# A new order of steps in the four later chunks and in the front of an mLSTM cell with an exact-GELU feed-forward

## The chip, the cores and the metric

The kernel runs on one core of one Trainium2 chip. The metric is the device time of one execution in microseconds (us). A core has five engines with a queue each, which run in the order of their own queue and wait for each other through semaphores: TensorE (PE, with its weight loads listed as PEld), VectorE (DVE), ScalarE (ACT), GpSimd (POOL) and SyncE (SP), which here issues the DMAs.

## The reference

Two blocks follow each other. The first is an mLSTM cell over 4 batches, 8 heads, 768 steps and a head dimension of 40, the second a feed-forward with exact GELU over all 3072 tokens of 8 x 40 = 320 features and 2048 hidden features, in float32.

```python
for t in range(S):                                   # B=4, H=8, S=768, D=40
    m_new = np.maximum(f_gate[:, :, t] + m, i_gate[:, :, t])
    f_stab, i_stab = np.exp(f_gate[:, :, t] + m - m_new), np.exp(i_gate[:, :, t] - m_new)
    C = f_stab * C + i_stab * outer(v_t, k_t)
    n = f_stab * n + i_stab * k_t
    denom = np.maximum(np.abs(n . q_t), 1.0)
    y[:, :, t] = sigmoid(o_gate[:, :, t]) * (C @ q_t) / denom
x = y.transpose(0, 2, 1, 3).reshape(3072, 320)
h = x @ w_in                                         # 320 -> 2048
out = (0.5 * h * (1.0 + erf(h / sqrt(2)))) @ w_out   # 2048 -> 320
```

## The kernel before, in words

**Tiling.** The 768 steps are cut into six chunks of 128 steps for all four batches. Inside a chunk the recurrence is computed in matrix form: scores of queries and keys, weighed by a mask of decays, times the values, plus what the state carried over from the chunks before gives. The 512 tokens (4 x 128) of a chunk then go through the feed-forward: an up-projection into 16 rows of 128 hidden features each, GELU, and a down-projection that adds up 16 rows of products. Float32 products are taken as three faster products each (a rounded part, the rest against it, and a low part, `x_hi`, `x_rest`, `x_low`, and likewise for weights and for GELU's results). A row of the down-projection is 3 parts x 4 batches = 12 matmuls (line 991); the up-projection is lines 966 and 977.

**What sets the order.** The program is put under a manual schedule: steps are emitted by `play` from strings of words, and each engine runs its instructions in the order of emission. A word is a letter and, mostly, a number (a batch, a row or a quarter). There is one string for the front (`FRONT`: loading, the cells of chunks 0 and 1, the conversion and splitting of weights, and the feed-forward of chunk 0), one for chunk 1 (`SECOND`), one for chunks 2, 3 and 4 (`LATER`) and one for chunk 5 (`LAST`). While a later chunk's feed-forward runs on TensorE, the cell of the next chunk, and the masks and transposes of the one after it, are threaded between its products.

**Letters of a later chunk.** `U`, `u` up-projection of a quarter and its 64-row remainder; `g`n GELU of row n (ACT lines 984 and 985, then DVE lines 986 and 987); `d`n the products of row n; `E` the results of the chunk before (line 1015). Cell steps, with number 0 to 3 for the next chunk's batches and 4 to 7 for those of the chunk behind it: `M` mask (POOL line 474), `W` weights (exp, ACT line 500), `G` gate (ACT line 506), `D` weighed values `vw` (line 539), `K`, `Q` transposes of keys and queries (DVE line 512), `S` scores of two batches (PE line 568, DVE line 574), `C` reading the state for two batches (PE line 621), `h` updating it (PE line 632, DVE lines 639 and 647, POOL line 643), `V` values (PE line 674, DVE line 678), `Y` finish (DVE from line 685), `t` a copy that the transposes need (line 699), `X` transposes of y (PE line 708) with `x_hi` (ACT line 718), `R` the rest and low parts (DVE lines 727 and 728). `L`, `B`, `J`, `O`, `j`, `o` and `+` issue DMAs on SP; `Z`, `a`, `b` split weights.

**Letters of the front.** `K` and `J` are the two halves of converting a piece of weights (`K`: ACT lines 404 and 405; `J`: DVE lines 416 and 419 and the load of a later piece); `m w g t s c v y x` are mask, weights, gate, turn (transposes, PE line 530, copied by ACT line 533), scores (PE line 552, DVE line 555), carry (PE line 590), values (PE line 656), finish and transposes of y for chunk 0, `M W G T S C V Y X R` the same for chunk 1; `I4` sets four matmuls that keep the clock up, issued at the next bank that is not read; `A`, `U`, `f` are parts of chunk 0's up-projection, `i` the split of its weights (line 756), `u` of its x; `F` is the next row of chunk 0's products (line 888: four float32 matmuls, or 12 of the faster kind for a row whose GELU result was split by `z`, lines 873 to 875); `a`, `b` split the output weights (lines 935 and 943); `(`, `)`, `[`, `p`, `r`, `e` and `+` prepare chunk 2's keys and queries.

In the mechanism, a step waits where its operands or its buffer or bank are not ready, and everything behind it on the same engine waits with it. GELU's result `g_whole` has two buffers, so a row's GELU waits for the DVE's second operation of the row two before it. Scores of two batches (`S`) take the banks that the GELU of four rows has just read.

Of the kernel before, what the change touches and what calls it, by code (L numbers as in the profile page):

```python
# [23 lines left out]


FRONT = """
    O0 L0 k1 P0 E L1 L2 t0 P1 k7 K w0 g0 N s0 w1 O1 O3 D k4 t1 P2 w2 c0 v0 J y0 Q s1 L3 O2 K d w3 q t2 L4 P3 v1
    g1 c1 J y1 s2 K x0 t3 x1 v2 g2 O4 J B4 g3 c2 y2 s3 B5 K x2 K L5 J T0 K v3 A y3 M1 x3 c3 G0 M0 H O7 O6 O5 J
    J i5 u0 L6 u1 K W0 J W1 I4 A K S0 T1 C0 J i6 V0 i7 u2 G2 K U M2 L7 S1 J G1 K U i8 W2 J i9 C1 T2 K
    M3 f2 S2 V1 Y0 T3 J Y1 C2 e W3 K K K J S3 J C3 f3 K X0 J K R0 J K J V2 K Y2 J J K  # L30
    K V3 X1 J K r F J K (0 )0 F J K F K J F X2 G3 F J K F Y3 R1 J K F p + + + + J F J a10,2 b10,2 z10 a12 b12 F X3 z11 F a13,3 b13,3 z12 F z13 [1 F B8 z14 F B9 R2 z15 F R3 B10 B11 F a8 b8 a9 b9 F"""
CELL = "MWGVYXRKQDCSht"

HI_AT = {3: ("w_out3", 0), 8: ("w_out3", 2), 4: ("w_out0", 0), 5: ("w_out0", 1), 6: ("w_out2", 0), 7: ("w_out2", 1), 9: ("f0", 0)}
# [1 line left out]
for at, first, key in ((HI_AT, 10, "h0"), (LO_AT, 10, "h1"), (HI_AT, 13, "b0"), (LO_AT, 13, "b1"), (HI_AT, 0, "b2"), (LO_AT, 0, "b3")):  # L36
    at.update((first + i, (key, i)) for i in range(3))
LATER = """
 U0 u0 E0 E1 E2 E3 K1 Q1 L2 D0 D1 C0 h0 M2 M3 g0 g1 g2 g3 +
 U1 u1 g4 d0 g5 d1 g6 d2 g7 S0 d3 K2 Q2 L3 W2 W3 G0 G1 G2 G3 +  # L40
 U2 V0 V1 u2 g8 d4 g9 K3 Q3 B4 B5 J0 J1 d5 g10 d6 g11 S2 L4 d7
 U3 u3 + M4 M5 Y0 Y1 D2 D3 K4 W4 W5 g12 t0 d8 g13 t1 d9 g14 X0 X1 R0 d10 g15 R1 C2 h2 O0 O1 d11 V2 V3 Y2 t2 B6 J2 d12 Y3 t3 Q4 L5 B7 d13 X2 X3 R2 d14 R3 d15 + O2 O3"""

SECOND = """
 U0 u0 j2 o0 o1 K1 Q1 L2 M0 M1 D0 D1 W0 W1 a0,3 b0,3 a3 b3 a4,2 b4,2 a6,2 b6,2 C0 h0 M2 M3 g0 g1 g2 g3 o2 o3 + +
 U1 u1 Z Z Z g4 d0 g5 d1 g6 d2 g7 S0 d3 K2 Q2 L3 W2 W3 G0 G1 G2 G3 Z Z +
 U2 V0 V1 u2 + g8 d4 g9 K3 Q3 B4 B5 J0 J1 d5 g10 d6 g11 S2 L4 d7
 U3 u3 + M4 M5 Y0 Y1 D2 D3 K4 W4 W5 g12 t0 d8 g13 t1 d9 g14 X0 X1 R0 d10 g15 R1 C2 h2 O0 O1 d11 V2 V3 Y2 t2 B6 J2 d12 Y3 t3 Q4 L5 B7 d13 X2 X3 R2 d14 R3 d15 + O2 O3"""

LAST = """  # L50
 U0 u0 E0 E1 E2 E3 g0 g1 g2 g3 U1 u1 g4 d0 g5 d1 g6 d2 g7 d3 
# [1056 lines left out]
```

## Time and profile before

| | us |
|---|---|
| median of 3 runs | 438.67 (437.14 to 439.19) |
| profiled execution, its own time | 438.46 |
| its span | 436.7 |
| TensorE busy | 427.3 (98%) |
| VectorE busy | 296.0 (68%) |
| ScalarE busy | 277.3 (63%) |
| GpSimd busy | 48.8 (11%) |
| granted TensorE clock | 1.00 of full speed |

The profile is of one execution; its times are counted from the start of the span. A line of the profile's page or of a query names the kernel's line, the engine, the operation and the tiles (out<-in). "waited for" and "<-" name what ended an idle time. "issue" is idle time for which the trace shows no cause. In the kernel's own terms the front takes up to about 118 us, the four chunks from there to about 380 us and the last chunk the rest.

### The profile page before, as it was taken

What the parts mean: (1) busy time and instruction counts of PE and PEld (TensorE: products, weight loads), DVE (VectorE), ACT (ScalarE), POOL (GpSimd) and SP (SyncE); (2) the same over time, 40 slices, a digit from 0 to 9 for tenths busy, and PEclk for the clock granted to TensorE, in tenths of its full rate; (3) what the DMA queues carried; (4) which work ended last, traced back from release to release, by engine and by line L of the source; (5) the groups of instructions that cost most, each with busy time, mean ns of one, the idle gap of its engine ahead of it and who ended that gap; (6) DMA issues with size and microseconds to landing.
All of it is one profiled execution on the core that took longest, in us unless ns stands there. A gap on an engine that the chain in (4) does not pass through costs nothing.

```text
span 436.7 us, 13291 instructions
## 1 busy us (share of the span) xinstructions
PE 427.3 (98%) x5472; PEld 374.6 (86%) x5472; DVE 296.0 (68%) x680; ACT 277.3 (63%) x595; POOL 48.8 (11%) x77
## 2 busy tenths in 40 slices
PE   8989999999999999999999999999999999999996
PEld 7777888877988899988899988899988889979986
DVE  8797687797888697747597747597746586533330
ACT  4989999856889985228785229785247715243441
POOL 3001030000430041030041030040010000000000
PEclk9999999999999999999999999999999999999999
DMA  7999994577791592662492653571561400010001
GB/s 151 220 214 243 233 256 87 138 211 179 229 154 56 106 176 60 115 179 50 84 187 42 123 158 60 117 134 32 110 156 17 62 2 2 22 42 2 1 2 60
DMA packets 162268, 48.83 MB, mean 112 GB/s; under 512 B 147776, under 2 KB 155232, under 8 KB 162208
## 3 DMA queue, kind: packets, MB, share of 16 engines
q1 hardware_dynamic: 161888, 47.65, 50.1%
q8 instruction: 43, 0.70, 0.6%
q10 hardware_dynamic: 320, 0.33, 0.2%
q14 instruction: 17, 0.14, 0.1%
HBM read 43.84 MB, written 9.37 MB: 122 GB/s over the span
## 4 chain that ended last, share of the span: by engine, by line
PE 73%; DVE 2%; ACT 2%; DMA 1%; issue 1%; ACTq 0%
PE po L991 31%; PE pu L966 24%; PE pu L977 7%; PE ps L568 3%; PE pf L621 2%; PE ph L674 1%; PE po L888 1%; PE po L674 1%; PE px L708 1%; DMA bits<-in_moe_w_out_dram 1%; PE pf L632 1%; DVE pow L416 1%; DVE w_out L419 0%; ACT w_out_part L935 0%; ACT g_part L873 0%
## 5 line engine op out<-in xcount | busy, mean ns | idle before, releaser
L991 PE MATMUL po<-w_out_part,g_parts 128*128 128x320 f32 x960 | 140.7, 303 | 0.0
L991 PEld LDWEIGHTS po<-w_out_part,g_parts 128*128 128x128 f32 x960 | 131.6, 189 | 5.9 <-issue 4.6
L986 DVE TENSOR_TENSOR g_parts<-g_whole,g_parts 128x512 fp32r<-128x512 f32 x80 | 57.0, 713 | 58.1 <-ACT g_parts L985 56.0
L984 ACT ACTIVATE g_whole<-pu 128x512 f32<-128x512 f32 x80 | 47.1, 589 | 74.2 <-PE pu L977 63.7
L985 ACT ACTIVATE g_parts<-g_whole 128x512 fp32r<-128x512 f32 x80 | 50.5, 631 | 8.3 <-PE po L991 5.1
L474 POOL TENSOR_SCALAR_AFFINE_SELECT W<-W 128x1024 f32<-128x1024 f32 (+2 forms) x20 | 21.7, 1088 | 189.2 <-DMA W<-M_d 154.4
L500 ACT ACTIVATE W<-W,aT 128x128 f32<-128x128 f32 x128 | 38.8, 389 | 0.3
L987 DVE CAST g_parts<-g_whole 128x512 fp32r<-128x512 f32 x80 | 36.2, 453 | 0.0
L699 ACT COPY far<-ob 128x128 f32<-128x128 f32 x16 | 4.6, 290 | 32.9 <-DVE ob L690 32.9
L966 PE MATMUL pu<-x_hi,w_in_hi 128*128 128x512 f32 x80 | 24.2, 384 | 0.0
L966 PE MATMUL pu<-x_hi,hi_first 128*128 128x512 f32 x80 | 24.0, 381 | 0.1
L966 PE MATMUL pu<-x_rest,hi_first 128*128 128x512 f32 x80 | 23.8, 379 | 0.0
L966 PE MATMUL pu<-x_rest,w_in_hi 128*128 128x512 f32 x80 | 23.8, 379 | 0.0
L966 PE MATMUL pu<-x_low,w_in_lo 128*128 128x512 f32 x80 | 23.8, 379 | 0.0
L966 PE MATMUL pu<-x_low,w_in 128*128 128x512 f32 x80 | 23.8, 379 | 0.0
L888 PE MATMUL po<-w_out,g 128*128 128x320 f32 x80 | 22.0, 432 | 0.0
L404 ACT ACTIVATE sig<-bits 128x320 f32<-128x320 f32 (+1 forms) x26 | 15.2, 586 | 10.4 <-issue 6.1
L574 DVE TENSOR_TENSOR W<-ps,W 128x256 f32<-128x256 f32 (+1 forms) x48 | 17.7, 414 | 4.2 <-PE ps L568 3.2
L888 PEld LDWEIGHTS po<-w_out,g 128*128 128x128 f32 x80 | 15.0, 190 | 5.9
L639 DVE TENSOR_TENSOR far<-pf,gT 128x164 f32<-128x164 f32 x32 | 8.4, 319 | 16.1 <-PE pf L632 11.7
L416 DVE SCALAR_TENSOR_TENSOR pow<-sig,pow 128x320 uint32<-128x320 uint32 (+1 forms) x26 | 15.4, 592 | 4.3 <-ACT pow L405 4.3
L1015 ACT ACTIVATE o_sb<-po 128x320 f32<-128x320 f32 x20 | 7.5, 443 | 16.7 <-PE po L991 16.7
(196 smaller groups left out, 778.9 us busy)
## 6 DMA issues: line engine op xcount, KB each, us to landing
W<-M_d SPq DMA_DIRECT2D x16, 512.0 KB, 6.5
bits<-in_moe_w_in_dram SPq DMA_DIRECT2D x20, 256.0 KB, 4.2
bits<-in_moe_w_out_dram SPq DMA_DIRECT2D x16, 320.0 KB, 4.6
blocks<-kq_d SPq DMA_DIRECT2D x32, 128.0 KB, 3.5
ob<-in_o_gate_dram SPq DMA_DIRECT2D x24, 160.0 KB, 4.1
out_dram<-o_sb SPq DMA_DIRECT2D x36, 80.0 KB, 2.0
wide<-M_d SPq DMA_DIRECT2D x4, 512.0 KB, 4.8
kq_d<-in_k_dram SPq DMA_DIRECT2D x6, 320.0 KB, 4.6
```

What stands on the lines that cost most here:

```text
L416: nc.vector.scalar_tensor_tensor(out=p, in0=s, scalar=3, in1=p, op0=OP.logical_shift_left, op1=OP.bitwise_or)
L474: nc.gpsimd.affine_select(out=x, in_=x, compare_op=OP.is_ge, fill=1.0e30, base=base, pattern=[[0, H], [1, x.shape[2]]], channel_multiplier=-1)
L500: nc.scalar.activation(out=W[n][:, h, :], in_=src, func=AF.Exp, scale=-1.0, bias=aT[:, self.c, r:r + 1])
L574: nc.vector.tensor_tensor(out=w[r, :, t], in0=ps[i][hip][r, :, t], in1=w[r, :, t], op=OP.mult)
L888: nc.tensor.matmul(to, xs[k][:, b * L:(b + 1) * L], w, start=(n == 0 and k == 0), stop=(n == NF - 1 and k + 1 == len(xs)), skip_group_chec ...
L966: nc.tensor.matmul(in_pairs(pus[i][e]), w3(at[k])[n][:, e, i * P:(i + 1) * P], in_turns(x3[n][:, k, :]), start=(n == 0 and k == 0), stop=F ...
L977: nc.tensor.matmul(in_pairs(pus[i][e]), w3(r)[n][h, p % 2, i * P:(i + 1) * P], in_turns(x3[n][h, NX, :]), start=False, stop=(n == 2), skip ...
L984: nc.scalar.activation(out=whole, in_=self.pus[n // 4][n % 4 // 2][n % 2], func=AF.Gelu)
L985: nc.scalar.activation(out=hi, in_=whole, func=AF.Copy, scale=PART)
L986: nc.vector.tensor_tensor(out=rest, in0=whole, in1=hi, op=OP.subtract)
L987: nc.vector.tensor_copy(out=low, in_=whole)
L991: nc.tensor.matmul(in_pairs(self.po[t]), x[:, t * L:(t + 1) * L], in_turns(w), start=(n == 0 and k == 0), stop=(n == NF - 1 and k == 2), s ...
```

## The change

Two of the strings get a new order from a given place on, and one throughout; no step is added or dropped, and no function changes.

- In the four later chunks the update `h2` is followed at once by the values `V3 V2` (before: `h2 O0 O1 d11 V2 V3`), the gelu `g15` and `R1` change turns, and the last transposes are spread, `d13 X2 d14 X3` in place of `d13 X2 X3 R2 d14 R3`, so that `R2 R3` come together. `Q3` and `K3` go ahead of `g9`; `Y1 D3 Y0` and `t1`, `t0` change turns.
- In chunks 2 to 4 also the first two quarters: the results of the chunk before (`E`) are spread between the steps, `D1 M2 D0 C0 M3 h0` replaces `D0 D1 C0 h0 M2 M3`, `S0` goes ahead of `g7`, and `G3 G1 G2 G0` ahead of `W3 W2`.
- The front is the same up to `v1 g1 c1 J y1 s2 K x0 t3 x1 v2 g2`; from there its cell steps, conversions, loads and splits come in another order. Among others `c2` follows `g2` directly, `I4` comes after `S0 C0`, `T2` before `i9`, and among the rows `F` the splits `z10`, `z11` and `z12` come one row earlier and the order of `Y3`, `R1`, `X2`, `X3` and of the copies `+` is new.

```diff
@@ -24,11 +24,12 @@
 
 
 FRONT = """
-    O0 L0 k1 P0 E L1 L2 t0 P1 k7 K w0 g0 N s0 w1 O1 O3 D k4 t1 P2 w2 c0 v0 J y0 Q s1 L3 O2 K d w3 q t2 L4 P3 v1
-    g1 c1 J y1 s2 K x0 t3 x1 v2 g2 O4 J B4 g3 c2 y2 s3 B5 K x2 K L5 J T0 K v3 A y3 M1 x3 c3 G0 M0 H O7 O6 O5 J
-    J i5 u0 L6 u1 K W0 J W1 I4 A K S0 T1 C0 J i6 V0 i7 u2 G2 K U M2 L7 S1 J G1 K U i8 W2 J i9 C1 T2 K
-    M3 f2 S2 V1 Y0 T3 J Y1 C2 e W3 K K K J S3 J C3 f3 K X0 J K R0 J K J V2 K Y2 J J K
-    K V3 X1 J K r F J K (0 )0 F J K F K J F X2 G3 F J K F Y3 R1 J K F p + + + + J F J a10,2 b10,2 z10 a12 b12 F X3 z11 F a13,3 b13,3 z12 F z13 [1 F B8 z14 F B9 R2 z15 F R3 B10 B11 F a8 b8 a9 b9 F"""
+    O0 L0 k1 P0 E L1 L2 t0 P1 k7 K w0 g0 N s0 w1 O1 O3 D k4 t1 P2 w2 c0 v0 J y0 Q s1 L3 O2 K d w3 q t2 L4 P3 v1 g1
+    c1 J y1 s2 K x0 t3 x1 v2 g2 c2 O4 J B4 y2 B5 s3 g3 K L5 J T0 x2 K K M1 v3 A y3 c3 M0 G0 x3 H J O6 O5 J O7 u0
+    L6 u1 K i5 W0 J W1 A K S0 C0 I4 T1 G2 J i6 u2 U i7 V0 K M2 S1 J G1 M3 L7 K U C1 i8 J W2 T2 i9 K f2 Y0 S2 V1
+    T3 J Y1 C2 K e W3 K J K S3 J C3 f3 K X0 J K J K K R0 J K V2 Y2 J J J K K V3 (0 X1 K F G3 J )0 J
+    K F J r F J F F X2 + R1 K K p F J Y3 + F + J z10 a12 K F a10,2 b10,2 J + b12 z11 F a13,3 b13,3 z12 F F X3 z13 F
+    B8 z14 F B9 R2 z15 F [1 R3 F a8 B10 B11 a9 b9 F b8"""
 CELL = "MWGVYXRKQDCSht"
 
 HI_AT = {3: ("w_out3", 0), 8: ("w_out3", 2), 4: ("w_out0", 0), 5: ("w_out0", 1), 6: ("w_out2", 0), 7: ("w_out2", 1), 9: ("f0", 0)}
@@ -36,16 +37,15 @@
 for at, first, key in ((HI_AT, 10, "h0"), (LO_AT, 10, "h1"), (HI_AT, 13, "b0"), (LO_AT, 13, "b1"), (HI_AT, 0, "b2"), (LO_AT, 0, "b3")):
     at.update((first + i, (key, i)) for i in range(3))
 LATER = """
- U0 u0 E0 E1 E2 E3 K1 Q1 L2 D0 D1 C0 h0 M2 M3 g0 g1 g2 g3 +
- U1 u1 g4 d0 g5 d1 g6 d2 g7 S0 d3 K2 Q2 L3 W2 W3 G0 G1 G2 G3 +
- U2 V0 V1 u2 g8 d4 g9 K3 Q3 B4 B5 J0 J1 d5 g10 d6 g11 S2 L4 d7
- U3 u3 + M4 M5 Y0 Y1 D2 D3 K4 W4 W5 g12 t0 d8 g13 t1 d9 g14 X0 X1 R0 d10 g15 R1 C2 h2 O0 O1 d11 V2 V3 Y2 t2 B6 J2 d12 Y3 t3 Q4 L5 B7 d13 X2 X3 R2 d14 R3 d15 + O2 O3"""
+ U0 E0 K1 E1 E2 Q1 E3 u0 L2 D1 M2 D0 C0 M3 h0 g0 g1 g2 g3 + U1 u1 g4 d0 g5 d1 g6 d2 S0 g7 K2 d3 Q2 L3 G3 G1 G2 G0 W3 W2
+ + U2 V0 V1 u2 g8 Q3 d4 K3 g9 B4 d5 B5 J0 J1 d6 g10 g11 S2 L4 d7 U3 + u3 M4 M5 D2 Y1 D3 Y0 K4 W4 W5 d8 g12 t1 g13 t0 d9 g14
+ X0 X1 R0 d10 R1 C2 h2 O0 g15 O1 V3 V2 Y2 d11 t2 B6 J2 d12 Y3 Q4 t3 L5 B7 d13 X2 d14 X3 R2 R3 + O2 O3 d15"""
 
 SECOND = """
- U0 u0 j2 o0 o1 K1 Q1 L2 M0 M1 D0 D1 W0 W1 a0,3 b0,3 a3 b3 a4,2 b4,2 a6,2 b6,2 C0 h0 M2 M3 g0 g1 g2 g3 o2 o3 + +
- U1 u1 Z Z Z g4 d0 g5 d1 g6 d2 g7 S0 d3 K2 Q2 L3 W2 W3 G0 G1 G2 G3 Z Z +
- U2 V0 V1 u2 + g8 d4 g9 K3 Q3 B4 B5 J0 J1 d5 g10 d6 g11 S2 L4 d7
- U3 u3 + M4 M5 Y0 Y1 D2 D3 K4 W4 W5 g12 t0 d8 g13 t1 d9 g14 X0 X1 R0 d10 g15 R1 C2 h2 O0 O1 d11 V2 V3 Y2 t2 B6 J2 d12 Y3 t3 Q4 L5 B7 d13 X2 X3 R2 d14 R3 d15 + O2 O3"""
+ U0 u0 j2 o0 o1 K1 Q1 L2 M0 M1 D0 D1 W0 W1 a0,3 b0,3 a3 b3 a4,2 b4,2 a6,2 b6,2 C0 h0 M2 M3 g0 g1 g2 g3 o2 o3 + + U1 u1 Z Z Z g4
+ d0 g5 d1 g6 d2 g7 S0 d3 K2 Q2 L3 W2 W3 G0 G1 G2 G3 Z Z + U2 V0 V1 u2 + g8 Q3 d4 K3 g9 B4 d5 B5 J0 J1 d6 g10 g11 S2 L4
+ d7 U3 + u3 M4 M5 D2 Y1 D3 Y0 K4 W4 W5 d8 g12 t1 g13 t0 d9 g14 X0 X1 R0 d10 R1 C2 h2 O0 g15 O1 V3 V2 Y2 d11 t2 B6 J2 d12 Y3 Q4
+ t3 L5 B7 d13 X2 d14 X3 R2 R3 + O2 O3 d15"""
 
 LAST = """
  U0 u0 E0 E1 E2 E3 g0 g1 g2 g3 U1 u1 g4 d0 g5 d1 g6 d2 g7 d3
```

## The prediction

> **What bounds the kernel now.** I read the page's busy times first, then the table by stage, then PE's waits ahead of 113 us, then the chain through one later chunk.
>
> ```profile
> PE 427.3 (98%) x5472; PEld 374.6 (86%) x5472; DVE 296.0 (68%) x680; ACT 277.3 (63%) x595; POOL 48.8 (11%) x77
> ```
> ```profile
> core 0: us, PE busy (x) PEld busy (x) DVE busy (x) ACT busy (x) POOL busy (x), PEclk, DMA share, GB/s
> 20.00:40.00 20.00, 18.15 (x361) 15.03 (x359) 18.05 (x48) 17.73 (x40) 0.00 (x0) 1.00 0.99 229
> 40.00:60.00 20.00, 19.62 (x210) 15.91 (x211) 14.86 (x25) 19.89 (x44) 3.31 (x3) 1.00 1.07 233
> ```
> ```profile
> 84.00:120.00 36.00, 35.35 (x281) 28.18 (x269) 30.44 (x64) 25.20 (x53) 4.77 (x5) 1.00 0.70 193
> ```
> ```profile
> 184.00:250.00 66.00, 66.00 (x931) 59.28 (x930) 44.96 (x106) 39.38 (x86) 10.53 (x14) 1.00 0.54 110
> ```
> TensorE sets the time: 98% busy, at a granted clock of 1.00 in every stage. The columns after the length are PE, weight loads, DVE, ACT, POOL. A later chunk (184 to 250) has no PE idle at all, so a new order there can save only what PE spends in its own switches; it can, however, create waits that are not there now. The front is different: between 20 and 40 PE is idle for 1.85 us, between 84 and 120 for 0.65, and between 40 and 60 ACT is full (19.89 of 20) and the DMA engines too (1.07).
>
> The waits of PE between 25 and 113 us, and the one DMA wait of ACT that bears on them (engine, line, what it waited for: us, times, longest):
> ```profile
> PE pf L590 <- DVE vw L539: 0.7, 1, 0.7
> PE po L888 <- DVE g_part L874: 0.6, 2, 0.4
> PE px L708 <- DVE y_rest L699: 0.5, 1, 0.5
> PE ps L552 <- ACT qT L533: 0.4, 1, 0.4
> ```
> ```profile
> ACT sig L404 <- DMA bits<-in_moe_w_in_dram: 1.0, 1, 1.0
> ```
> These 2.2 us are all that the front's order can win by visible waits. The change adds and removes no work: all matmuls, activations with their table loads, vector operations and DMAs are the same, in another order on each engine, so the sum below holds waits and switches only. It is made against the profiled execution's own 438.46 us (span 436.7 and 1.76 around it), 0.21 under the median of the three runs, 438.67.
>
> **Change, part 1: the tail of the four later chunks** (chunks 1 to 4, one text for chunk 1, one for 2 to 4). The chain of chunk 2 between the products of rows 8 and 15, and a run of three rows from chunk 4:
> ```profile
> 231.63 3.46 PE po L991 x24
> 235.09 0.66 PE px L708 x6
> 235.74 1.63 PE po L991 x12
> 237.38 1.07 PE pf L621 x64
> 238.45 0.74 PE pf L632 x32
> 239.19 1.83 PE po L991 x12
> 241.02 1.51 PE ph L674 x117
> 242.53 3.46 PE po L991 x24
> ```
> ```profile
> 246.69 3.26 PE po L991 x24
> ```
> ```profile
> 330.13 5.09 PE po L991 x36
> ```
> A row of products is 12 matmuls of L991: 1.63 us behind transposes (L708), 1.83 behind cell matmuls (L621, L632, L674). The 0.20 more is the switch. Before: rows 8-9, X0 X1, 10, read and update (C2 h2), 11, V2 V3, 12-13, X2 X3, 14-15. After: rows 8-9, X0 X1, 10, C2 h2 V3 V2, 11-12-13, X2, 14, X3, 15. One entry from cell matmuls goes: 1.83 + 3.46 + 3.26 = 8.55 becomes 5.09 + 1.63 + 1.63 = 8.35. The six transposes fall into two threes, which I cost at nothing. That is 0.20 a chunk, **0.8 us over four**; below, zero if the split transposes give it back, above, 1.2 if V behind h2 also loses a switch of 0.1.
>
> What waits for what: V3 and V2 now come one row (1.83 us) earlier. Their matmuls need W; what the DVE makes of them in place needs `far` of the update. The groups that carry this (all chunks; busy us, mean ns):
> ```profile
> L639 DVE TENSOR_TENSOR far<-pf,gT 128x164 f32<-128x164 f32 x32 | 8.4, 319 | 16.1 <-PE pf L632 11.7 <-PE pf L621 4.4
> L727 DVE TENSOR_TENSOR x_rest<-px,x_hi 128x384 fp32r<-128x384 f32 x20 | 11.0, 552 | 2.9 <-ACT x_hi L718 2.8
> L728 DVE CAST x_low<-px 128x384 fp32r<-128x384 f32 x20 | 10.9, 547 | 0.0
> L718 ACT ACTIVATE x_hi<-px 128x384 fp32r<-128x384 f32 x20 | 8.9, 487 | 2.1 <-PE px L708 1.9
> L987 DVE CAST g_parts<-g_whole 128x512 fp32r<-128x512 f32 x80 | 36.2, 453 | 0.0
> ```
> Four `far` operations are 1.3 us of DVE, beside V's own 1.51 us on PE, and the DVE is freer there than before: gelu row 15's two vector operations (0.65 for L986, shown below, and 0.45) move behind them, and they are not wanted before row 15's product, at least two rows (3.4 us) later. What V adds in place is only read by the finish Y2, which therefore starts no later, and X3 follows it as before. At the chunk's end only row 15 (1.63 us) lies between X3 and the next up-projection. Its operands follow in the order of their use, x_hi after 0.49 us, x_rest after 0.55 more and x_low after 0.55 more: 1.59. They are there when row 15 ends; I cost this at nothing, and without the cover it would be the second and third of these, 1.1 us.
>
> There is one wait which no dependency explains, in chunk 1's V2 V3:
> ```profile
> 176.69 0.35 issue
> ```
> "issue" means that PE waited for nothing that the trace records. It is 0.35 us once in four chunks; it may move or go (-0.35), or the longer stream of small matmuls (96 + 128, now without products between) may bring it into each of four chunks (+1.4). I take 0.
>
> [...]
>
> **Part 2: third quarter (U2).** The transposes K3 and Q3 (L512, on DVE) move from behind gelu row 9's vector work to ahead of it. DVE, ACT, POOL and PE of chunk 2:
> ```profile
> 219.31 0.70 DVE L512 STREAM_TRANSPOSE kT<-blocks 128x512 f32<-128x512 f32 x1
> 219.94 0.67 DVE L512 STREAM_TRANSPOSE qT<-blocks 128x512 f32<-128x512 f32 x1
> 220.53 0.65 DVE L986 TENSOR_TENSOR g_parts<-g_whole,g_parts 128x512 fp32r<-128x512 f32 x1
> ```
> ```profile
> 221.44 1.58 DVE L986 TENSOR_TENSOR g_parts<-g_whole,g_parts 128x512 fp32r<-128x512 f32 x1
> ```
> ```profile
> 219.55 0.58 ACT L984 ACTIVATE g_whole<-pu 128x512 f32<-128x512 f32 x1
> ```
> ```profile
> 221.27 1.20 POOL L474 TENSOR_SCALAR_AFFINE_SELECT W<-W 128x1024 f32<-128x1024 f32 x1 [25.43 <-ACT g_parts L985]
> ```
> ```profile
> 221.56 1.57 PE L568 MATMUL ps<-qT,kT 64*64 64x128 f32 x64
> ```
> The gelu of row 11 (219.55) reuses the buffer that row 9's L987 frees; that comes later by the two transposes' pitch, 220.53 - 219.31 = 1.22 us. So it ends at 219.55 + 0.58 + 1.22 = 221.35, and S2, whose first matmuls reuse the banks that the gelus empty, begins at 221.56. A margin of 1.4 us becomes 0.2. That costs nothing by these rows; but a DVE operation beside the POOL's mask took 1.58 instead of 0.65, so if the mask moves onto row 9's pair, S2 stalls by up to 2 x 0.93 - 0.2 = 1.7 us a chunk. I put +0.3, a sixth of that, for one chunk of four being touched lightly.
>
> [...]
>
> **Part 3: first and second quarters.** S0 goes ahead of row 7's vector work, the G steps change turns with no added table load, and on POOL the masks M2, M3 go ahead of the state's decay in h0.
> ```profile
> 192.11 0.93 POOL L643 TENSOR_TENSOR state<-state,dec 128x164 f32<-128x164 f32 x2 [8.21 <-PE pf L621]
> ```
> ```profile
> L474 POOL TENSOR_SCALAR_AFFINE_SELECT W<-W 128x1024 f32<-128x1024 f32 (+2 forms) x20 | 21.7, 1088 | 189.2 <-DMA W<-M_d 154.4
> ```
> POOL was idle for 8.21 us before that decay, and two masks of 1.20 fit in it if their loads have landed; the profile's largest wait of POOL is for these loads (154.4 of 189.2 us idle before L474), so this is not sure. If a load lands less than 1.2 us ahead of the decay, the decay is late by up to one mask. Zero, bounded by 0 and +1.2 in all.
>
> **Part 4: the front.** C2 now follows g2 directly, so vw (L539) runs on the DVE ahead of J's pair: the 0.7 at L590 goes. The y_rest wait (0.5) moves with s3 and x2. But all ACT work between the bits it waits 1.0 us for at 32 us and T1's copies at 55 is the same set, and ACT is full in that stretch; S1 waits for the last of those copies (L552 on L533 in the waits above). So what PE wins before 55 us becomes a longer wait at S1. I take 0, between -1.2 (if ACT's bits come earlier too) and +0.6 (the loads of that stretch are DMA-bound and change turns with the gate loads O4 to O7).
>
> From 84 us the F rows have the split rows 10 to 12. PE and the chain:
> ```profile
> 107.50 0.93 PE L888 MATMUL po<-w_out_part,g_part 128*128 128x320 f32 x4
> 108.70 3.53 PE L888 MATMUL po<-w_out_part,g_part 128*128 128x320 f32 x24 [0.27 <-DVE g_part L874]
> 112.61 0.68 PE L888 MATMUL po<-w_out_part,g_part 128*128 128x320 f32 x3 [0.38 <-DVE g_part L874]
> ```
> ```profile
> 102.29 2.98 issue
> ```
> 28 matmuls took 112.61 - 107.50 = 5.11 us; at 5.09 / 36 = 0.141 each they need 3.96. So 1.15 us is lost, more than the 0.6 which the waits show. The cause lies earlier: ACT stood 2.98 us after 102.29 because the next weight conversion needs a DVE step that is queued behind Y3, itself behind a gate on ACT, and R1. After the change these come apart: R1 goes behind an earlier J, Y3 behind four more rows, and the splits z10, z11, z12 each move one row earlier. With that idle gone, what was ready at 112.61 is ready at 109.6, and PE without waits would want it at 107.50 + 24 x 0.141 = 110.9. The wait goes whole: **-1.15**, at least -0.6 (what shows as waits). What would be late next is chunk 1's first up-projection, whose X3 comes after row 10 instead of before row 11; its cover is five rows of 12 x 0.141 = 1.70 us.
>
> Sum: -0.8 - 1.15 + 0.3 + 0 = -1.65 us; 438.46 - 1.65 = 436.8.
>
> **The rivals.** (a) *Faster:* the early front's 1.2 us are kept, the tails give 1.2 and the idle issue goes: -1.2 - 1.2 - 1.15 - 0.35 = -3.9, **434.6**. For it: two waits go for certain. Against: ACT at 19.89 of 20.
>
> (b) *No gain:* the split rows find another late input (weights' conversion is DMA-fed; the DMA share is 0.70 there) and keep 0.6 of their loss, and the split transposes eat the tails' 0.8: -0.5, **438.0**. In this case the change moves work but not PE.
>
> (c) *Slower:* S2 waits for row 11's gelu in all four chunks, since the mask's release by its DMA falls on row 9's DVE pair. At one operation stretched whole and one by half, 1.4 - 0.2 = 1.2 us each, four times, +4.8; with the -1.15 and -0.8 kept that is +2.85, **441.3**. It decides from a delay of 0.2 us upward, and outweighs the gains from 0.5 us a chunk. For it: the margin is one short operation. Against: the mask began 2 us behind row 9's place (221.27 against 219.31) in chunk 2.
>
> **How the numbers follow.** The forecast has 0.47, (a) 0.24, (b) 0.14, (c) 0.15. About 0.5%, 2.19 us, is what a measurement of this kernel can tell from no change: faster below 436.3, slower above 440.65. The forecast's own range is 435.6 to 438.0 (tails 0 to 1.2, split rows 0.6 to 1.15, S2 0 to 1); a third of it lies below 436.3. Faster: 0.24 + 0.16 = 0.40. Same: 0.31 + 0.14 = 0.45. Slower: 0.15. The range for 8 in 10 takes in (a) and stops short of (c)'s middle: 434.5 to 440.6.
>
> **What would show it.** Right: no wait of L888 on L874 near 107 us and 28 split matmuls in about 4.0; a run of 36 L991 in each tail; a longer wait at S1's L552 on ACT; S2 (L568) starting without idle. Wrong: any wait ahead of L568 on L984, of L643's state ahead of PE, of L674 behind h2, or "issue" inside the small matmuls; and above all a later chunk whose PE busy falls short of its length.

## The result, and the profile after

The changed kernel takes 439.96 us (median of 14 runs, 438.73 to 442.19), the kernel before 438.46 (14 runs beside them, 436.9 to 439.46): a ratio of 1.0042, 95% interval 1.0026 to 1.0057. It is slower by 1.5 us, less than 0.5%. The forecast was 436.8. The profiled execution of the changed kernel took 438.73 us, the fastest of the 14; so its trace shows only 0.27 us of the 1.5 directly, and two further executions below show where time over that can go.

The busy times and the table by stage of the changed kernel (columns as before: PE, weight loads, DVE, ACT, POOL, clock, DMA share, GB/s):

```profile
PE 425.7 (97%) x5472; PEld 374.5 (86%) x5472; DVE 294.4 (67%) x680; ACT 278.0 (64%) x595; POOL 49.5 (11%) x77
```
```profile
20.00:40.00 20.00, 18.58 (x364) 15.38 (x361) 18.15 (x48) 17.91 (x40) 0.00 (x0) 1.00 0.99 236
40.00:60.00 20.00, 18.83 (x208) 15.45 (x206) 13.22 (x24) 19.85 (x44) 3.42 (x3) 1.00 1.07 240
...
84.00:120.00 36.00, 36.00 (x301) 29.25 (x301) 32.41 (x66) 26.46 (x54) 5.06 (x5) 1.00 0.77 198
...
184.00:250.00 66.00, 65.14 (x926) 58.62 (x925) 44.96 (x106) 39.24 (x86) 10.65 (x14) 1.00 0.53 109
```

Two rows have changed places. From 84 to 120 PE is now busy for all 36.00 us (35.35 before), and the later chunk that had no idle at all (66.00 of 66) now lacks 0.86. PE's waits between 25 and 113 us, and then between 165 and 380 us in the changed kernel and in the one before:

```profile
PE ps L552 <- ACT qT L533: 0.9, 1, 0.9
PE px L708 <- DVE y_rest L699: 0.4, 1, 0.4
PE ph L656 <- DVE W L555: 0.2, 1, 0.2
```
```profile
PE ph L674 <- issue: 2.5, 3, 0.9
```
```profile
PE ph L674 <- issue: 0.3, 1, 0.3
```

The first two views are of the changed kernel, the third is of the one before. The wait of L590 is gone and that of the scores (L552) is longer, as the forecast had it; the wait of L888 is gone. New are three waits of 0.8 to 0.9 us inside the values (L674), without a releaser: "issue" waits. The chain of the changed kernel's chunk 2, in the same form as before:

```profile
234.41 1.63 PE po L991 x12
236.05 1.07 PE pf L621 x64
237.12 0.74 PE pf L632 x32
237.86 1.10 PE ph L674 x94
238.97 0.86 issue
239.83 0.49 PE ph L674 x29
240.32 5.09 PE po L991 x36
245.41 0.33 PE px L708 x3
245.73 1.63 PE po L991 x12
247.37 0.33 PE px L708 x3
247.69 1.63 PE po L991 x12
```

The three rows in one run (5.09) and the single rows behind transposes (1.63) are what the forecast added up; the 0.86 us in the middle of V is not. The lengths of the parts, taken from the starts of the matmuls (S1: first score of batches 0 and 1 at L552; F rows: first L888 to the first up-projection of chunk 1; a chunk: from its first up-projection to the next chunk's), in us:

| profiled execution | S1 at | F rows | chunk 1 | chunk 2 | chunk 3 | chunk 4 | last chunk |
|---|---|---|---|---|---|---|---|
| before | 55.15 | 33.16 | 65.87 | 65.24 | 65.56 | 63.87 | 53.42 |
| changed | 55.45 | 31.98 | 65.42 | 65.94 | 65.97 | 64.33 | 53.43 |
| difference | +0.30 | -1.18 | -0.45 | +0.70 | +0.41 | +0.46 | 0 |

The differences add up to +0.24 us, which is that of the spans. What the front won, chunks 2 to 4 gave back.

### The profile page after: what moved, and what is told of

Read it like the earlier page. It is cut to its first block, busy times and chain, and to the rows that moved or that the text cites. A ratio compares the mean times of both kernels' runs of the same rounds, so it can differ in the third digit from the quotient of the medians.

```text
span 436.9 us, 13265 instructions
## 1 busy us (share of the span) xinstructions
PE 425.7 (97%) x5472; PEld 374.5 (86%) x5472; DVE 294.4 (67%) x680; ACT 278.0 (64%) x595; POOL 49.5 (11%) x77
## 4 chain that ended last, share of the span: by engine, by line
PE 86%; ACT 6%; DVE 4%; DMA 2%; issue 1%; SPq 1%; ACTq 0%; DVEq 0%
PE po L991 31%; PE pu L966 24%; PE po L888 7%; PE pu L977 7%; PE ps L568 3%; PE pu L787 2%; PE pf L621 2%; PE px L708 2%; ACT W L500 2%; PE ph L674 1%; PE po L674 1%; PE pf L632 1%; ACT pow L405 1%; PE pu L818 1%; DMA bits<-in_moe_w_in_dram 1%
## 5 line engine op out<-in xcount | busy, mean ns | idle before, releaser
L986 DVE TENSOR_TENSOR g_parts<-g_whole,g_parts 128x512 fp32r<-128x512 f32 x80 | 55.5, 693 | 54.7 <-ACT g_parts L985 52.9
L987 DVE CAST g_parts<-g_whole 128x512 fp32r<-128x512 f32 x80 | 36.3, 453 | 0.0
L574 DVE TENSOR_TENSOR W<-ps,W 128x256 f32<-128x256 f32 (+1 forms) x48 | 17.7, 413 | 8.3 <-PE ps L568 8.0
L888 PE MATMUL po<-w_out,g 128*128 128x320 f32 x80 | 21.9, 432 | 0.0
L888 PEld LDWEIGHTS po<-w_out,g 128*128 128x128 f32 x80 | 15.0, 190 | 6.0
L405 ACT ACTIVATE pow<-bits,low_bits 128x320 uint32<-128x320 uint32 (+1 forms) x26 | 17.5, 674 | 0.0
```

The lines of the kernel that those rows point to most:

```text
L405: nc.scalar.activation(out=p, in_=lo, func=AF.Relu, scale=0.9 * 2.0 ** -29, bias=low_bits)
L574: nc.vector.tensor_tensor(out=w[r, :, t], in0=ps[i][hip][r, :, t], in1=w[r, :, t], op=OP.mult)
L888: nc.tensor.matmul(to, xs[k][:, b * L:(b + 1) * L], w, start=(n == 0 and k == 0), stop=(n == NF - 1 and k + 1 == len(xs)), skip_group_chec ...
L986: nc.vector.tensor_tensor(out=rest, in0=whole, in1=hi, op=OP.subtract)
L987: nc.vector.tensor_copy(out=low, in_=whole)
```

## The theories

Three theories were put to the test. A, code supply: TensorE's instructions arrive in blocks, and read, update and values in a row (C2 h2 V3 V2: 64 + 32 + 128 matmuls, each with its weight load, 448 instructions in 3.3 us) use a block up before the next one is there. C, a hidden wait: a bank, weights or a vector result for V is late without a mark in the trace. B, the front: it hands the chunks a worse state. What the DMA view shows in chunk 3 of the changed kernel speaks for A. These are the chain there, the one packet of the instruction queue (q8; packets, MB, share) between 302.75 and 303.8 us, and all DMA traffic between 303.8 and 305.4:

```profile
303.06 0.74 PE pf L632 x32
303.80 0.71 PE ph L674 x58
304.51 0.85 issue
305.36 0.93 PE ph L674 x54
```
```profile
q8 instruction: 1, 0.02, 5.7%
```
```profile
DMA packets 0, 0.00 MB, mean 0 GB/s; under 512 B 0, under 2 KB 0, under 8 KB 0
```

By the packets' own records in the trace, a block of 16 KB starts at 303.03, just as the update (L632) begins, and its packet takes 0.96 us; PE stops at 304.51, with no packet starting in the meantime, and goes on at 305.36, 2.33 us after the fetch began. That distance is 2.34, 2.21, 2.33 and 2.25 us in chunks 1 to 4, with waits of 0.10, 0.86, 0.85 and 0.76. In the whole span there are 43 such packets for 11,085 records of TensorE (matmuls, weight loads and the sequencer's steps), one per 258.

The expectations below count S1 and the start of a fetch 0.24 us earlier than the profile's scale does: their 54.9 and 55.2 us for S1 are 55.15 and 55.45 here, and their 2.5 us for a fetch are 2.2 to 2.3.

## The experiments

**e1_front: the new front, the old chunk orders.**
```diff
 FRONT  = (new order)
-LATER, SECOND = (new orders)
+LATER, SECOND = (old orders)
```


> The new front with the old orders of the four later chunks. [...] Theory B (the loss comes from the front: later loads or buffers that reach chunk 1 and on in a worse state): slower than before by about 1.5 us, with issue waits in the chunks although their order is the old one.

Measured: 438.38 us against 438.61, ratio 1.0000 (0.9987 to 1.0012). The chunks have one issue wait, 0.27 us in chunk 1, so B falls. But the gain that A leads one to expect, 0.9 us (the 1.18 of the F rows less the 0.30 at S1), did not come, although the F rows take 31.98 us as in the changed kernel: S1 is at 56.41, 0.96 later than there. ACT's wait near 32 us for `bits` (the weights as loaded, line 404) was 1.7 us in this execution and not 1.0, which can be 0.7 of it.

**e2_late_front: the old front up to word 138, the new rest, the old chunk orders.**
```diff
-FRONT = (before)
+FRONT = (before, to "f3 K X0 J K") + (changed, from there on)
```


> The old front up to the first f3 K X0 J K (138 words), the new order of its rest, the old orders of the later chunks. If the 0.30 us at S1 are due to the order between 25 and 55 us and the 1.18 us in the F rows to the rest alone: 1.2 us faster than before, S1 at 54.9 us and the F rows 32.0 us long. If the rest needs what the early part moved: the F rows keep part of their 33.2 us and the gain is under 0.6.

Measured: 437.83 us, ratio 0.9980 (0.9967 to 0.9994); F rows 31.98 us. The late front is a gain of 0.8 by itself, and needs nothing of the early part. S1 was at 55.92 here with the old early part (55.15 before), with a wait for bits of 1.6 us.

**e3_row_between: d11 back between update and values.**
```diff
-R1 C2 h2 O0 g15 O1 V3 V2 Y2 d11 t2
+R1 C2 h2 O0 g15 O1 d11 V3 V2 Y2 t2
```


> The changed kernel with one row of products (d11) put back between the update h2 and the values V3 V2 in all four chunks. Theory A: the row's 24 instructions take 1.6 to 1.8 us, in which the next block of code arrives; the issue waits of 0.86, 0.85 and 0.76 us go, one of 0.35 may stay in chunk 1; each chunk pays 0.2 us for one more switch; in all 1.5 to 1.8 us faster than the changed kernel, about 0.6 to 1.0 faster than before. Theory C (a hidden wait: bank, weights or a vector result for V that the trace doesn't show): the wait goes as well, since V comes 1.8 us later; this run doesn't tell A from C.

Measured: 437.46 us, ratio 0.9971 (0.9955 to 0.9987), 2.5 us under the changed kernel's median. Two issue waits of 0.2 us are left, in chunks 1 and 2. Expected were 1.5 to 1.8. One word's place turns the slower kernel into one 1.15 us faster than before (438.61 beside it).

**e4_shift and e8_shift_clean: the same orders, with 68 instructions more ahead of them.** The first swaps warm-up matmuls at the start; the second adds 17 small ones where PE waits for a load anyway.
```diff
-    fill(76); warm(4)
+    fill(95); warm(2)          # e4_shift
+    ... if n == 7: fill(17)    # e8_shift_clean, inside warm(n)
```


> The changed kernel with its orders as they are; only the warm-up at the very start has 19 small filler matmuls more and 2 larger ones fewer, about the same time and 68 TensorE instructions more. Theory A: all later blocks of 256 instructions begin 68 instructions earlier in the chunks. By the rows of the changed kernel the waits of 0.1, 0.86, 0.85 and 0.76 us in chunks 1 to 4 become about 0.85, 0.55, 0 and 0: another pattern, 1.2 us less in all. Theory C (a hidden wait on bank, weights or a vector result): the same three waits of 0.8 us in chunks 2 to 4 and the same time.

> The changed kernel with its orders as they are; 17 small filler matmuls (68 TensorE instructions) are put into the first microseconds where TensorE waits 0.97 us for a load anyway (behind k7), so nothing later should move but the places where blocks of code begin. The shift before this one had moved the whole front by 2 us. Theory A: the front as in the changed kernel (S1 at 55.2 us plus what ACT's wait for bits at 32 us is longer), and the pattern of issue waits of the first shift, 1.3, 1.2, 0 and 0 in chunks 1 to 4. Theory C: 0.1, 0.86, 0.85 and 0.76 as in the changed kernel.

Measured: 442.04 us, ratio 1.0071 (1.0039 to 1.0104), and 439.58 us, ratio 1.0026 (1.0007 to 1.0046). In the chains of the first, the issue waits in chunks 1 and 2 are these, and in 3 and 4 there is none:
```profile
175.83 1.34 issue
...
242.49 1.19 issue
```
And of the second, likewise only chunks 1 and 2:
```profile
173.93 1.20 issue
...
239.83 1.22 issue
```
No order was touched, and the pattern went from 0.1, 0.86, 0.85, 0.76 to 1.3, 1.2, 0, 0, the chunks that A had named. C falls: a bank or a result that is late would be late in chunks 3 and 4 too. The sizes were wrong (0.85 and 0.55 were expected in e4), so the sum stayed at about 2.5 and no time was won.

A count in the traces leaves no room for C. Number TensorE's records of one trace (matmuls, weight loads and the sequencer's steps) from 0 in the order of their starts. Twelve traces have issue waits of PE of 0.1 us and more, 25 in all, under every order here, the one before included. Each of the 25 ends at a record whose number leaves 193 or 194 when divided by 256. In before it is record 4802, in the changed kernel 4802, 6594, 8385 and 10177. A bank or a result that is late would not keep to such a count.

e4's added 2 us have another cause, which stays open: its front stood at ACT for
```profile
ACT sig L404 <- DMA bits<-in_moe_w_in_dram: 3.0, 1, 3.0
```
instead of 1.0, and S1 was at 57.51; in e8 it was 1.1, and S1 at 55.56, near the 55.45 of the changed kernel.

**e5_halves: fewer instructions at the same place.** V2 and V3 in halves of 64 columns.
```diff
-                    for r in quarters:
+                    for r in quarters if b < 2 else halves:
```


> The changed kernel, but the values of the last two batches (V2, V3) are taken in halves of 64 columns instead of quarters of 32: half the instructions (64 matmuls in place of 128 a chunk) at the same place in the order, same results. The nearest matmul of this shape, the carry at L590, comes every 0.029 us, so the values should take 1.9 us instead of 1.5. Theory A (code supply): read, update and values are then 320 instructions in 3.7 us instead of 448 in 3.3, no 256 of them pass in under 2.5 us except around the read, so the issue waits fall from 2.57 us in all to 0.5 or less; the sum is 4 x 0.4 - 2.1 = 0.5 us faster than the changed kernel. Theory C (a hidden wait on bank, weights or a vector result): the waits of 0.8 us stay or shrink by 0.4 at most, and the time is the same or longer.

Measured: 437.99 us, ratio 0.9991 (0.9981 to 1.0002), against 1.0042 of the changed kernel. PE has no wait at all from 119 to 380 us. The chain of chunk 1:
```profile
171.78 0.74 PE pf L632 x32
172.52 1.87 PE ph L674 x64
174.39 3.73 PE po L991 x26
```
The values take 1.87 us for 64 matmuls instead of 1.49 for 128, slower as work, faster as a kernel. The chunks are 65.38, 65.34, 65.46 and 63.99 us, 1.5 less in all than the changed kernel's, where 0.5 was expected: all 2.57 us of waits went instead of 2.1, and the slower values cost 1.1 us instead of 1.6. The instruction queue of the changed kernel and of this one, over the whole span:
```profile
q8 instruction: 43, 0.70, 0.6%
```
```profile
q8 instruction: 41, 0.67, 0.6%
```
For 512 TensorE instructions less (4 chunks x 64 matmuls with a weight load each) there are two packets less, 256 instructions to a packet.

**e6_values_up: the kernel before with this one move.**
```diff
-C2 h2 O0 O1 d11 V2 V3 Y2
+C2 h2 O0 O1 V2 V3 Y2 d11
```


> The kernel before with one edit: V2 V3 and Y2 go ahead of d11, straight behind the update, in all four later chunks. If this one move makes the loss: issue waits inside or right behind the values of up to 1.3 us in each chunk, 2.5 us in all (0.35 before), 0.2 us a chunk won back from the switch, so 1 to 2 us slower than before. If the loss needs the rest of the change (the gelu moved behind, the transposes ahead of it): within 0.5 us of before, with no new wait.

Measured: 441.92 us against 438.59, ratio 1.0077 (1.0059 to 1.0094), worse than expected. PE's waits from 119 to 380 us:
```profile
PE ph L674 <- issue: 2.6, 3, 1.1
PE po L991 <- issue: 0.7, 1, 0.7
PE ph L674 <- DVE x_low L728: 0.5, 1, 0.5
```
This move alone makes the loss, and more: in the profiled execution the four chunks are 2.7 us longer than before; the front, whose order is the same, is 0.8 longer. The third row is in chunk 4, where the values wait for R1's second operation, which comes behind g15's vector work on the DVE. The change has R1 ahead and g15 behind, and its trace shows no such wait.

**e7_late_and_row: e2's front with e3's chunks; e12_row_again the same once more; e11_old_third_quarter with the old order of U2.**
```diff
 e7, e12: FRONT of e2, chunk orders of e3
-U2 ... g8 Q3 d4 K3 g9 B4 d5 B5 J0 J1 d6 g10 g11 S2
+U2 ... g8 d4 g9 K3 Q3 B4 B5 J0 J1 d5 g10 d6 g11 S2     # e11 beside it
```


> The old front up to the first f3 K X0 J K and the new order of its rest, with the new orders of the later chunks but d11 between the update and the values. The sum of the parts measured so far: 0.8 us from the late front and 0.95 us from the chunks (what the row between won beyond the whole new front), 436.9 against 438.6 of before, a ratio of 0.996. If both parts draw on the same slack, no better than 437.5.

> The faster version (late front, d11 between update and values), but with the old order of the third quarter: g9 ahead of the transposes K3 and Q3. Two further executions of the changed kernel had shown chunk 3 at 67.1 and 67.9 us instead of 66.0, with S2 waiting for row 11's GELU behind those transposes and masks on POOL. If that place costs time in part of the executions here too: chunk 3 never over 65.5 us, the highest times fall, median 0.2 to 0.5 us under the same version with the new third quarter. If it needs the later arrival that the issue waits and the new early front cause: the same median within 0.3 us.

> The faster version itself once more, on the same chip as the run before it, to compare the two and to repeat its ratio: 0.996 of before if the first measurement holds (436.5 against 438.6).

Measured: e7 436.50 us, ratio 0.9964 (0.9949 to 0.9979); e12 437.25, 0.9961 (0.9944 to 0.9978); e11 436.79, 0.9958 (0.9940 to 0.9977). Each is about 0.4% faster than before, and so faster than both kernels. In e7 the chunks took 65.76 (with an issue wait of 0.27), 65.06, 65.06 and 63.57 us. In e12 chunk 2 took 66.24, with this wait (its lines are numbered two higher, L986 is the GELU):
```profile
PE ps L570 <- ACT g_whole L986: 0.6, 1, 0.6
```
e11 has no wait of PE from 119 to 380 us, and on the same chip a median 0.46 us lower than e12; the intervals overlap, so the gain from the old third quarter is likely and not shown.

**e9_again and e10_again: two more executions of the changed kernel.**

> The changed kernel once more, for a second profiled execution: the first one took 438.73 us, the fastest of 14, and the median is 439.96. Theory A1: the waits for code vary from run to run with the time that a fetch takes; in an execution of about 440 us the four issue waits sum to 3.5 us or more instead of 2.57, at the same places. Theory F: the fetch waits are 2.6 again and the rest lies in the front, where ACT waits for bits at 32 us: S1 later than 55.2 by what the execution is longer.

> As the run before: a third profiled execution of the changed kernel. Theory A1: issue waits in the same chunks, their sum rises with the time of the execution. Theory F: their sum stays at 2.6 and S1 moves.

Measured: 441.08 and 441.97 us, against 437.44 for one run of before on that chip. Neither theory holds alone. S1 came at 56.75 and 56.52 (waits for bits of 1.9 and 1.7 us); the issue waits of L674 sum to 2.7 and 3.3 us; and chunk 3 took 67.12 and 67.89 us instead of 65.97, for the most part from a third cause. In e10, PE, ACT, DVE and POOL around S2:
```profile
288.39 1.55 PE L568 MATMUL ps<-qT,kT 64*64 64x128 f32 x58 [0.48 <-ACT g_whole L984]
...
292.27 0.45 PE L966 MATMUL pu<-x_hi,hi_first 128*128 128x512 f32 x1 [0.51 <-DVE W L574]
```
```profile
287.74 0.60 ACT L984 ACTIVATE g_whole<-pu 128x512 f32<-128x512 f32 x1 [2.19 <-DVE g_parts L987]
```
```profile
284.57 0.71 DVE L512 STREAM_TRANSPOSE qT<-blocks 128x512 f32<-128x512 f32 x1 [0.41 <-DMA blocks<-kq_d]
...
286.37 1.33 DVE L987 CAST g_parts<-g_whole 128x512 fp32r<-128x512 f32 x1
```
```profile
286.34 1.09 POOL L474 TENSOR_SCALAR_AFFINE_SELECT W<-W 128x1024 f32<-128x1024 f32 x1 [27.37 <-DMA W<-M_d]
```
S2 waits for row 11's GELU, which waits 2.19 us for row 9's L987. That operation is behind Q3 and K3, of which Q3 waited 0.41 us for its load, and it took 1.33 us beside a mask that began at 286.34; the same cast took 0.42 at 283.74, with no mask beside it. So beside a mask this cast, which reads one tile, took longer too, as L986, which reads two, did in the kernel before (1.58 instead of 0.65). In e9 S2 starts without idle, but the vector work on its scores (L574) ends late, and the next up-projection waits 0.86 us for it.

## Why the prediction was wrong, step by step

**The step that failed** is the one that took 0 for the "issue" wait in part 1. It named the mechanism's place ("the longer stream of small matmuls ... may bring it into each of four chunks (+1.4)") and then priced it at nothing; no run shows that 0. Measured: 2.57 us against 0.35, so +2.2 in the profiled execution, and 2.7 and 3.3 in the two others. The bound was also too low: it took the one wait seen, 0.35, as the size of each (and from one chunk to four that would add 1.05, not 1.4). With these waits all but gone (e3), the new order is 1.15 us faster than before, not far from the 1.65 of the forecast. The trace of before held a sign of it: the 0.35 us ended at 177.04, and the last block's fetch had begun at 174.67, 2.37 us earlier; at 448 instructions in 3.3 us, a block of 256 is used up in less than that wherever it starts between the read's beginning and the values'.

**Runs of products beside this stream.** In chunks 2 to 4 of the changed kernel PE goes through the rows of products, where 24 instructions take 1.63 us, without an "issue" wait of 0.1 us or more; the waits stand inside the values, 0.86, 0.85 and 0.76 us (the second at 304.51). In the 25 waits, PE stopped for a block whose fetch had begun only 67 to 268 records earlier (67, 206, 177 and 215 in the four chunks of the changed kernel).

**Split rows, -1.15:** right. -1.18 measured, and 31.97 or 31.98 us in each of the twelve traces with the new late front. In the timeline of the changed kernel, PE goes through the split rows without idle (transposes of X3 between):
```profile
107.45 2.03 PE L888 MATMUL po<-w_out_part,g_part 128*128 128x320 f32 x12
...
109.57 3.64 PE L888 MATMUL po<-w_out_part,g_part 128*128 128x320 f32 x25
```

**Tails, -0.8 in all:** near in sum, and by luck. Without their issue waits the four chunks are 0.20, 0.16, 0.44 and 0.30 us shorter, 1.10 in all; 0.3 of chunk 3's is another wait which the execution of before had in its third quarter. But the reason was wrong: in chunks 2 to 4 the merged rows brought nothing (0.17 in chunk 1). e7, which keeps d11 apart, has 65.06 us in chunk 2 against the 65.08 of the changed kernel without its wait, 65.06 against 65.12 in chunk 3, and 63.57 against 63.57 in chunk 4. Its chain in chunk 2:
```profile
237.83 1.83 PE po L993 x12
239.65 1.38 PE ph L676 x116
241.03 3.46 PE po L993 x24
```
These are 6.67 us. In the changed kernel the values behind the update took 1.10 + 0.49, without the wait, and the three rows 5.09, together 6.68: the 0.20 that the rows save is paid by the values. What e7 has over the kernel before at this place is values of 1.38 us instead of 1.51 (in e12 they took 1.59).

**Early front, 0:** nearly right in the profile, +0.30 at S1, with the gain at L590 turned into a longer wait there, as forecast. The old early front fared better in the medians: e2 is 0.55 us under e1, and e7 0.96 under e3, which ran on another chip (0.3 by the ratios to before). How much of that is the order and how much the wait for bits, which went from 1.0 to 1.9 us between executions of the same order, stays open.

**S2, +0.3, and rival (c):** in the profiled execution the margin was 0.55 us in chunk 2, where 0.2 had been worked out:
```profile
219.08 0.60 ACT L984 ACTIVATE g_whole<-pu 128x512 f32<-128x512 f32 x1 [0.77 <-DVE g_parts L987]
```
```profile
220.23 1.57 PE L568 MATMUL ps<-qT,kT 64*64 64x128 f32 x64
```
The GELU ends 0.55 us ahead of S2, and nothing was lost. In e10 and e12 the rival came true in one chunk, and not in four: S2 waited 0.48 and 0.55 us for row 11's GELU, and the chunk was 1.9 and 1.2 us longer than in the changed kernel and in e7 (0.3 of e10's is a longer issue wait). In e9 and e4 S2 itself did not wait, but the up-projection behind it did, 0.86 and 0.41 us. The prediction had the mask in it, not the transposes' own wait for their load (0.41 us in e10, 1.41 in e12).

Against the first profiled execution of the changed kernel, e9's span is 2.36 us longer, of which 1.30 had come by S1 and 1.15 lie in chunk 3; e10's is 3.27 longer, 1.07 by S1, 0.57 in chunk 2 and 1.92 in chunk 3. That the 1.2 us between the fastest execution and the median have the same sources is likely and not shown.

**The forecast's own range**, 435.6 to 438.0: the terms named beside it (tails 0 to 1.2, split rows 0.6 to 1.15, S2 0 to 1) add up to 436.1 to 438.9, so it was drawn too low at both ends.

## What to carry to other kernels

Count instructions per microsecond, not only busy time: where small matmuls (each with its weight load) followed each other here without products between, 448 instructions in 3.3 us, TensorE stood for up to 1.4 us with a block of 256 instructions used up, and went on 2.2 to 2.9 us after the packet of the next one began. One row of slower products between (e3, e7) left 0.45 and 0.27 us of the 2.57, and fewer and larger matmuls, even at 1.87 us instead of 1.49 (e5), none. A wait that the trace lays to nothing deserves a look at the instruction queue's packets before it is priced at zero, and adding some dozens of instructions far ahead (68 in e4 and e8) tells a wait for code from a wait for data. Read two or three executions of a kernel whose margins are under 0.5 us before trusting one.

## What the runs showed of the hardware

In the 25 waits, PE went on 2.2 to 2.5 us after the last 16 KB packet of the instruction queue began where that packet took 0.9 to 1.0 us, and 2.6 to 2.9 us after where it took 1.4 (2.74 in e4's chunk 2, 2.93 in e6's chunk 1). These waits appear in the profiles as "issue" on a matmul with no releaser (0.85 us at 304.51). Where they fell went by the number of instructions ahead (record 193 or 194 past a multiple of 256, 25 times of 25), so that an edit in the first 8 us (e4, e8: 68 instructions) moved waits at 174 to 370 us. What the four matmuls of `I4` do for the clock no run shows: the granted clock was 1.00 in the profiled executions of both kernels.
